# Pooled attention and a gated MLP on one core: K's left-over rows in one transfer, V's beside them at half the width

## The chip, the cores and the metric

The kernel runs on one core of one Trainium2 chip. The time is the device time of one execution in microseconds; a kernel is judged by the median of its runs, and one execution is taken apart with the hardware profiler. Engines: PE (matrix products, with weight loads on PEld), DVE (VectorE), ACT (ScalarE), POOL (GpSimd), SP (which issues nearly all the DMAs). Each engine works through its own list of instructions in a fixed order.

## The reference

All inputs are float32 but `w_in` and `w_out`, which are float64. B = 8 batches, H = 8 heads, S = 576 positions, D = 64.

```
k_p = k.reshape(B, H, 72, 8, D).mean(axis=3)         # eight positions pooled into one
v_p = v.reshape(B, H, 72, 8, D).mean(axis=3)
scores = (q @ k_p.T) / sqrt(D)                       # 576 x 72 for each head
attn = softmax(scores)
x = (attn @ v_p) as [B, S, H * D]                    # 512 columns

h = gelu_tanh(x @ w_in)                              # 1024 columns
u, v = h[..., :512], h[..., 512:]
v_n = (v - mean(v)) / sqrt(var(v) + 1e-6) * g_ln
v_s = einsum('ts,bsd->btd', w_sg, v_n) + b_sg        # w_sg is 576 x 576, over the positions
out = x + (u * v_s) @ w_out
```

## The kernel before

**Products.** Each float32 operand of a product in the second half is split into a high and a low float32r part (`xhl` holds both for x, `vhh` and `vhl` for v, `wih` and `wil` for `w_in`, `woh` and `wol` for `w_out`, `wsh` and `wsl` for `w_sg`, `ah` and `al` for the transposed softmax, `ghi` and `glo` for the gated product), and three of the four cross products are formed. A split is a cast on ACT or DVE and a subtraction on DVE or POOL. The float64 weights are cut into such pairs by integer operations on the raw words (`step_w`: tiles `raw`, `top`).

**Pooling.** The 72 pooled keys of a pair of heads are 144 rows of 8 x 64 numbers: 128 fill the partitions (`kvraw`, two transfers a batch for K and two for V, pooled into `kp` and `vp`), 16 are left over. The four pairs' left-over rows go into a tile of their own, `left`, and are pooled into `lp`. Eight values are summed in `psum8`, either by one reduction of DVE over the whole row, or by three additions of POOL, each over half the length of the one before: 512, 256 and 128 numbers for `kvraw` and for `left` (two halves side by side). K and V of the first two batches are pooled by PE instead (`pool8`), but not their left-over rows. V's left-over means are multiplied by a mask of heads into `left` again (or, for the first two batches, into the tile `vl`), and are split into `vl` from there.

**Scores.** K's means are turned and written, scaled, into `kbd`, a tile with the two heads of a pair on the block diagonal: for batches 0 and 1 by PE transposes, later by DVE transposes (`y`), a round trip through DRAM (`kfar`) and five ACT operations. PE multiplies `kbd` by `qT`; DVE takes the maxima (`nmax`), ACT the exponentials with their sums (`e`, `ssum`), DVE scales `e`, which goes transposed into `ah` and `al` for the product with V.

**Order.** The work of a batch is cut into steps, and a table, `PROLOGUE`, lists which step issues its next piece: `K1+2` is step K, part 1, of batch 2. A and B load K and V, E the left-over rows, C loads q; K and P pool K and V (K2 the left-over rows and `kbd`, P2 V's mask and splits), Q makes `qT`, S scores and softmax, T and L the transposed softmax, V the product with V, H the v half of `x @ w_in` with its norm, U the u half, W the spatial gate, O the product with `w_out`, X and Z the output; small letters are the splits of the weights. A second table, `OTHER`, names operations that go to the other of two engines. The rule for sums is

```
def psum8(o, t, key):
    if key not in OTHER:  # three additions on GpSimd
        ...
    nc.vector.tensor_reduce(...)  # else one on VectorE
```

with `k31` for the second half of K from batch 3 on, `k20` for the first of batch 2, `l1` and `l2` for the left-over rows of batches 1 and 2 (`l3` from there on). For copies a key in `OTHER` means DVE instead of ACT (`K00` for pooled K of batch 0, `Q02` for `qT`, `T00` for `ah`, `s1` for `wsh`, `H23` for `vhh`), for low parts of v (`H20`) DVE instead of POOL, and for `xta`, a copy of x for the H step (`X20`), POOL instead of ACT.

**The end.** The last 64 positions of the last batch are formed apart, in `step_X`: two halves of 256 columns, 12 products each, an addition of x on DVE, and a store, the first on the SP queue and the second on ACT's.

Of the kernel before, what the change touches and what calls it, by code (L numbers as in the profile page):

```python
# [24 lines left out]
Q1+0 Q2+0 v0 S0+0 S1+0 v0 v1 Q2+0 S1+0 C3+0 S0+0 S1+0 Q3+0 Q3+0 S2+0 lo0 v1 S0+0 S2+0 o1 S1+0 o0 A0+1 K1+1 o1 S2+0
S3+0 T0+0 B0+0 S3+0 o0 K1+1 S3+0 P0+0 E0+1 S2+0 S2+0 S3+0 lv1 S1+0 T0+0 S3+0 v2 P1+0 ls0 K0+1 P2+0 L0+0 o1 lu0 v3 K0+1
v2 v3 o1 s0 T1+0 K2+1 L0+0 s0 B0+1 s0 v3 V0+0 s4 T1+0 V1+0 v2 C0+1 V0+0 s4 T2+0 V1+0 s1 C1+1 K2+1 s4 s3 s1 v3 T2+0 s1
V0+0 Q0+1 K2+1 T3+0 V2+0 s3 v2 u1 u1 T3+0 V2+0 V3+0 S0+1 o0 C2+1 s2 Q1+1 B1+1 V3+0 V2+0 V1+0 u0 S1+1 o0 s2 V3+0 S0+1
u1 S0+1 s3 lu1 S1+1 s2 S1+1 H2+0 Q2+1 u1 S0+1 H0+0 u0 P0+1 S1+1 u0 H0+0 S2+1 P0+1 u0 H2+0 V1+0 H0+0 S2+1 u3 V2+0 C3+1
S2+1 V0+0 H2+0 P1+1 u3 lo1 S1+1 U1+0 U0+0 H2+0 H2+0 S0+1 H0+0 H0+0 V3+0 U1+0 H2+0 u2 U0+0 o2 H3+0 H0+0 Q3+1 S2+1 C1+2  # L30
H4+0 u2 A0+2 u3 u2 H3+0 P1+1 S3+1 o2 H4+0 T0+1 A1+2 H4+0 S3+1 o2 S3+1 u3 H1+0 u2 S3+1 P2+1 P2+1 U3+0 o2 S3+1 H1+0 S2+1
T0+1 T0+1 L0+1 P2+1 P2+1 U2+0 C0+2 L0+1 K1+2 H4+0 T1+1 L0+1 V0+1 T1+1 H1+0 E0+2 U3+0 H3+0 K0+2 H4+0 T1+1 V0+1 V1+1
B0+2 B1+2 H3+0 H1+0 T2+1 V1+1 T2+1 H1+0 H1+0 T3+1 T2+1 U2+0 Q1+2 V2+1 H3+0 T3+1 H3+0 H4+0 H4+0 P1+2 V1+1 P0+2 T3+1
# [901 lines left out]
```

## Time and profile before

| | |
|---|---|
| median of three runs | 562.36 us (561.85, 562.36 and one of 3028.21) |
| the profiled execution, whole | 560.36 us |
| its span from first to last instruction | 558.7 us |
| instructions in it | 10694 |
| granted PE clock | 1.00 in every stretch |
| busy: PE, DVE, ACT, POOL | 538.1, 435.2, 330.6, 260.8 us |
| moved by DMA | 68.38 MB, 122 GB/s over the span |

A row of the timeline gives start, duration, engine, line, operation, what it writes and reads with shapes, and in square brackets the idle time before it with what ended it. A row of the groups gives line, engine, operation, shapes, count, then busy us and mean ns of one, then idle before. Shapes are partitions x elements. `xN` at the end of a timeline row stands for N such instructions in a row, with their time together. Lines are those of the kernel that ran.

### The profile page before, as it was taken

The numbers are of one execution on the slowest core, as the hardware profiler recorded it, in microseconds if no ns is written. First come the engines' busy times: TensorE is split into PE (matmuls) and PEld (weight loads), VectorE is DVE, ScalarE is ACT, GpSimd is POOL, SyncE is SP. The second block draws the span as 40 slices with busy tenths as digits, with TensorE's granted clock in tenths as the row PEclk, the third lists the DMA queues.
The fourth block names the chain that finished last, engine by engine and source line by source line (L and its number), as shares of the span: only waits on it lengthen the run. The fifth ranks groups of instructions, "written<-read, shape, count | busy, mean of one in ns | idle before, by whom it ended". The sixth has DMA issues, their size and how long they took to land.

```text
span 558.7 us, 10694 instructions
## 1 busy us (share of the span) xinstructions
PE 538.1 (96%) x3677; PEld 508.7 (91%) x3677; DVE 435.2 (78%) x644; ACT 330.6 (59%) x1077; POOL 260.8 (47%) x322
## 2 busy tenths in 40 slices
...
GB/s 246 315 298 164 93 120 76 69 145 122 158 147 90 93 155 146 138 111 134 166 104 158 86 177 162 119 48 151 122 169 99 95 44 83 78 59 2 32 13 106
DMA packets 186470, 68.38 MB, mean 122 GB/s; under 512 B 150576, under 2 KB 170800, under 8 KB 186416
## 3 DMA queue, kind: packets, MB, share of 16 engines
...
HBM read 48.20 MB, written 19.46 MB: 121 GB/s over the span
## 4 chain that ended last, share of the span: by engine, by line
PE 78%; DVE 9%; ACT 4%; SPq 3%; DMA 3%; issue 1%; POOL 0%; DVEq 0%; ACTq 0%; POOLq 0%
PE mps L139 66%; PE aps L139 12%; SPq L240 3%; ACT e L564 2%; DMA kvraw<-in_k 1%; ACT L207 1%; DVE vg L739 1%; DVE bst L733 1%; DVE al L649 0%; DMA al<-tfar 0%; DVE top L237 0%; DMA lfar<-y 0%; DVE e L223 0%; DVE raw L228 0%; DVE wsl L320 0%
## 5 line engine op out<-in xcount | busy, mean ns | idle before, releaser
L564 ACT ACTIVATE e<-aps,nmax 128x72 f32<-128x72 f32 x280 | 85.0, 354 | 6.3 <-DVE nmax L545 6.2
L139 PE MATMUL mps<-xhl,wih 128*128 128x288 f32 x512 | 88.2, 294 | 0.0
L139 PE MATMUL mps<-wih,xhl 128*128 128x512 f32 x256 | 84.7, 396 | 0.6 <-DVE wsl L320 0.3
L139 PEld LDWEIGHTS mps<-xhl,wih 128*128 128x128 f32 x512 | 75.5, 188 | 1.0
L237 POOL TENSOR_TENSOR glo<-u,ghi 128x576 fp32r<-128x576 f32 x29 | 42.4, 1478 | 69.9 <-ACT ghi L214 35.5
L564 ACT ACTIVATION_READ_ACCUMULATOR e<-aps,nmax 128x1 f32 x280 | 67.4, 242 | 0.0
L237 POOL TENSOR_TENSOR xhl<-x,xhl 128x576 fp32r<-128x576 f32 x30 | 43.8, 1471 | 41.9 <-ACT xhl L692 37.6
L139 PEld LDWEIGHTS mps<-wih,xhl 128*128 128x128 f32 x256 | 48.1, 188 | 11.1 <-ACT u L771 0.7
L139 PE MATMUL mps<-wsh,vhl 128*128 128x288 f32 x256 | 55.1, 296 | 0.3 <-DVE vhl L237 0.3
L139 PE MATMUL mps<-xhl,wil 128*128 128x288 f32 x256 | 54.8, 295 | 0.0
L139 PE MATMUL mps<-wsl,vhh 128*128 128x288 f32 x256 | 54.8, 295 | 0.0
L139 PE MATMUL mps<-wsh,vhh 128*128 128x288 f32 x256 | 54.7, 295 | 0.0
L139 PE MATMUL mps<-ghi,woh 128*128 128x288 f32 (+1 forms) x232 | 51.8, 302 | 0.0
L139 PE MATMUL mps<-ghi,wol 128*128 128x288 f32 (+1 forms) x232 | 50.8, 298 | 0.0
L139 PE MATMUL mps<-glo,woh 128*128 128x288 f32 (+1 forms) x232 | 50.8, 298 | 0.0
L139 PE MATMUL mps<-wil,xhl 128*128 128x512 f32 x128 | 50.1, 391 | 0.0
L785 DVE SCALAR_TENSOR_TENSOR mps<-mps,gcol,bbc 128x576 f32<-128x576 f32 x32 | 26.2, 819 | 27.6 <-PE mps L139 27.6
L237 POOL TENSOR_TENSOR vhl<-vg,vhh 128x512 fp32r<-128x512 f32 x25 | 34.6, 1389 | 23.5 <-DVE vhh L212 18.6
L736 POOL TENSOR_TENSOR rstd<-mv,eps 128x1 f32<-128x1 f32 (+1 forms) x40 | 13.0, 325 | 68.8 <-DVE mv L734 65.5
L646 ACT CAST ah<-al 128x640 fp32r<-128x640 f32 x24 | 17.5, 731 | 41.6 <-DMA al<-tfar 37.9
L139 PEld LDWEIGHTS mps<-wsh,vhl 128*128 128x128 f32 x256 | 41.1, 188 | 0.6 <-DVE vhl L237 0.6
L139 PEld LDWEIGHTS mps<-wsh,vhh 128*128 128x128 f32 x256 | 41.2, 188 | 0.0
...
## 6 DMA issues: line engine op xcount, KB each, us to landing
...
```

The lines of the kernel that those rows point to most:

```text
L139: nc.tensor.matmul(o, lhsT, rhs, start=start, stop=stop)
L207: nc.scalar.activation(early, eps[:, 0:1], func)
L237: (nc.vector if key in OTHER else nc.gpsimd).tensor_tensor(o, x, y, op=op)
L240: queue.dma_start(o, i)
L564: nc.scalar.activation(e[:, i, h], slots[i][:, h], AF.Exp, bias=nmax[:, i, h:h + 1], **acc)
L646: nc.scalar.copy(ah, al)
L733: nc.vector.bn_stats(bst, vg)
L736: nc.gpsimd.tensor_tensor(rstd, mv[:, 1:2], eps[:n, 1:2], op=ALU.add)
L739: nc.vector.scalar_tensor_tensor(vg, vg, mv[:, 0:1], rstd.broadcast_to([n, DF2]), op0=ALU.subtract, op1=ALU.mult)
L785: nc.vector.scalar_tensor_tensor(vs, vs, gcol[:, d:d + 1], bbc.rearrange("p (a n) -> p a n", a=2), op0=ALU.mult, op1=ALU.add)
```

## The change

**Left-over rows.** `left` is [128, 1, 512] instead of [128, 2, 512]. K's 64 rows of a batch come in one transfer to partitions 64 to 127, V's in two transfers of 32 rows to partitions 0 to 31 and 32 to 63; before, each of the two had two transfers of 32 rows, side by side in the same partitions. `psum8` of them covers 128 partitions, with one row of 512 numbers in each instead of two rows in 64 partitions: additions of 256, 128 and 64 numbers. The transposes and the DRAM trip of `lp` are half as wide (128x64), `kbd` of batches 0 and 1 takes one ACT operation for the left-over part instead of two, V's mask two POOL operations of 32x256 in every batch instead of one of 32x512 from batch 2 on.

**Last rows.** In `step_X` each half of the columns has a PSUM tile of its own, and the first half is added and stored ahead of the second half's products.

**Order.** `PROLOGUE` is another list from its start to where batches 2 and 3 meet, and differs further in the last output steps only; `OTHER` is another list altogether.

```diff
...
-A0+0 K0+0 A1+0 E0+0 K0+0 lv0 K1+0 v1 v0 K2+0 K1+0 K2+0 K2+0 v1 C0+0 v0 Q0+0 C1+0 Q0+0 S0+0 A1+1 S0+0 C2+0 B1+0 Q1+0
...
+A0+0 K0+0 A1+0 E0+0 lv0 C0+0 v0 K1+0 C2+0 K2+0 K1+0 K0+0 K2+0 v1 K2+0 C1+0 v0 Q0+0 Q0+0 v1 S0+0 Q1+0 Q2+0 S0+0 v1 S0+0
...
-G01 G10 G23 H13 H23 Q01 Q02 Q03 V02 V12 W00 W10 W13 X02 X03 X10 X12 X13 X21 X22 c21 c22 g00 g10 g12 g13 g14 g21 g22
-h01 k31 l1 l2 o0d o2a o2m o3m p30 p31 u0m u1m u2a u2d u3a u3d u3m v0m v1m v2a v2d v2m v3a x11
+G00 G12 G23 H01 H02 H10 H11 H12 H20 H22 K00 Q01 T00 V01 V03 W00 W02 W03 W13 X00 X03 X11 X12 X13 X20 X22 X23 c21 c22
+g11 g13 g22 h00 h11 h12 k20 o0m o1a o1d o1m o2d o2m o3d o3m p30 p31 s1 s2 u1d u2a u2d u2m u3m v0m v1d v2m x01 x12
...
     nc.gpsimd.affine_select(out=head[:, 1:2], in_=head[:, 1:2], compare_op=ALU.is_ge, fill=0.0, base=-SP,
                             pattern=[[0, 1]], channel_multiplier=1)
-    pick = const.tile([96, 2, NL], F32, name="pick")
-    mask = const.tile([96, 2, 2], F32, name="mask")
+    pick = const.tile([64, 2, 2 * NL], F32, name="pick")
+    mask = const.tile([64, 2, 2], F32, name="mask")
     nc.gpsimd.memset(pick, 1.0 / POOL)
     nc.gpsimd.memset(mask, 0.0)
-    sl = pick[64:96]
-    nc.gpsimd.affine_select(out=sl, in_=sl, compare_op=ALU.is_equal, fill=0.0, base=0,
-                            pattern=[[-1, 2], [-2, NL]], channel_multiplier=1)
-    nc.vector.tensor_reduce(out=mask[64:96, :, 1], in_=sl, axis=AX.X, op=ALU.add)
+    nc.gpsimd.affine_select(out=pick, in_=pick, compare_op=ALU.is_equal, fill=0.0, base=0,
+                            pattern=[[-1, 2], [-2, 2 * NL]], channel_multiplier=1)
+    nc.vector.tensor_reduce(out=mask[:, :, 1], in_=pick, axis=AX.X, op=ALU.add)
     kbd = const.tile([P, G, 2 * SP], F32, name="kbd")
     nc.gpsimd.memset(kbd, 0.0)
     vbh = const.tile([P, G, P], F32R, name="vbh")
...
     nc.gpsimd.tensor_copy(swap[:, 0:P // 2], ident[:, P // 2:P])
     nc.gpsimd.tensor_copy(swap[:, P // 2:P], ident[:, 0:P // 2])
     lp = const.tile([P, 2, D], F32, name="lp")
-    nc.gpsimd.memset(lp[0:64], 0.0)
+    nc.gpsimd.memset(lp[:, 1], 0.0)
     def turn(ps, src):
...
     def load_left(b):
-        t = per.tile([P, 2, POOL * D], F32, name="left")
-        for p0, src in ((96, k), (64, v)):
-            for gp in range(2):
-                load(t[p0:p0 + 32, gp], keys(src[b])[2 * gp:2 * gp + 2, P:2 * SP].rearrange("g r f -> r g f"))
+        t = per.tile([P, 1, POOL * D], F32, name="left")
+        load(t[64:P, 0], keys(k[b])[:, P:2 * SP].rearrange("g r f -> r g f"))
+        for gp in range(2):
+            load(t[32 * gp:32 * gp + 32, 0], keys(v[b])[2 * gp:2 * gp + 2, P:2 * SP].rearrange("g r f -> r g f"))
         st["left", b] = t
     def load_q(b, g):
...
                 psum8(kp, st.pop(("kv", b, 0, i)), f"k{min(b, 3)}{i}")
             return
         st["lp", b] = lp
-        psum8(lp[64:P], st["left", b][64:P], f"l{min(b, 3)}")
+        psum8(lp[:, 0:1], st["left", b], f"l{min(b, 3)}")
         yield
         kp = st.pop(("kp", b))
         c = D ** -0.5 / POOL
         if b not in BY_PE:
-            t = ring(per, [P, 2, 6, 32], "y", 2)
-            for n0, x in ((0, kp), (G, lp)):
+            t = ring(per, [P, 2, G + 1, 32], "y", 2)
+            for n0, x in ((0, kp), (G, lp[:, 0:1])):
                 nc.vector.transpose(t[:, :, n0:n0 + x.shape[1]].rearrange("p f g j -> p g f j"),
                                     x.rearrange("p g (f k) -> p g f k", k=32))
-            far = hbm.tile([P, 2, 6, 32], F32, name="kfar")
+            far = hbm.tile([P, 2, G + 1, 32], F32, name="kfar")
             load(far, t)
             yield
             far = far.rearrange("(q k) f g j -> k f q (g j)", k=32)
...
             for f in range(2):
                 r = slice(32 * f, 32 * f + 32)
                 load(kt[r], far[:, f, :, 0:P])
-                load(kl[r], far[:, f, 3, P:P + 64])
+                load(kl[r].rearrange("k (q j) -> k q j", q=2), far[:, f, 2:4, P:P + 32])
             yield
             kt = kt.rearrange("p q (g j) -> p g q j", g=G)
             m = SP - 64
...
             nc.scalar.mul(kbd[0:D, :, 64:SP], kt[:, :, 2, 0:m], c)
             nc.scalar.mul(kbd[D:P, :, SP:96], kt[:, :, 2, m:32], c)
             nc.scalar.mul(kbd[D:P, :, 96:P], kt[:, :, 3], c)
-            nc.scalar.mul(kbd[D:P, :, P:2 * SP].rearrange("p (f g) r -> p f g r", g=2),
-                          kl.rearrange("p (f r g) -> p f g r", f=2, g=2), c)
+            nc.scalar.mul(kbd[D:P, :, P:2 * SP], kl.rearrange("p (r g) -> p g r", g=G), c)
             return
         ps = atile()
         for g in range(G):
...
         main = ps[0:D, 0].rearrange("p (g j) -> p g j", g=G)
         nc.scalar.mul(kbd[0:D, :, 0:SP], main[:, :, 0:SP], c)
         nc.scalar.mul(kbd[D:P, :, SP:P], main[:, :, SP:P], c)
-        for gp in range(2):
-            nc.scalar.mul(kbd[D:P, 2 * gp:2 * gp + 2, P:2 * SP],
-                          ps[D * gp:D * gp + D, 1, 96:P].rearrange("p (r g) -> p g r", g=2), c)
+        nc.scalar.mul(kbd[D:P, :, P:2 * SP], ps[0:D, 1, 64:P].rearrange("p (r g) -> p g r", g=G), c)
     vb = {b: per.tile([P, G, P], F32, name="vb", tag=("vht", "al")[b]) for b in WHOLE}
...
                 psum8(vp, st.pop(("kv", b, 1, i)), f"p{min(b, 3)}{i}")
             return
         vp = st.pop(("vp", b))
-        vlp = st.pop(("lp", b))[64:96]
+        vlp = st.pop(("lp", b))[0:64, 0:1]
         left = st.pop(("left", b))
-        v32 = left[64:96, :, 0:4 * D].rearrange("p g (a d) -> p g a d", a=4)
+        v32 = left[64:96, 0].rearrange("p (g a d) -> p g a d", g=2, a=4)
         for h in range(2):
             nc.scalar.mul((vb[b] if b in WHOLE else vbh)[:, :, D * h:D * h + D], vp, head[:, h:h + 1])
-        heads = mask[64:96].rearrange("p g h -> p (g h)").unsqueeze(1).unsqueeze(3)
-        if b in TURNED:
-            for gp in range(2):
-                nc.gpsimd.tensor_tensor(st["vl", 0][64 + 32 * gp:96 + 32 * gp, gp:gp + 1],
-                                        vlp[:, gp:gp + 1].unsqueeze(2).broadcast_to([32, 1, 4, D]),
-                                        heads.broadcast_to([32, 1, 4, D]), op=ALU.mult)
-            if b in WHOLE:
-                return
-        else:
-            nc.gpsimd.tensor_tensor(v32, vlp.unsqueeze(2).broadcast_to([32, 2, 4, D]),
-                                    heads.broadcast_to([32, 2, 4, D]), op=ALU.mult)
+        heads = mask.rearrange("p g h -> p (g h)").unsqueeze(1).unsqueeze(3)
+        for gp in range(2):
+            r = slice(32 * gp, 32 * gp + 32)
+            nc.gpsimd.tensor_tensor(st["vl", 0][64 + 32 * gp:96 + 32 * gp, gp:gp + 1] if b in TURNED else v32[:, gp:gp + 1],
+                                    vlp[r].unsqueeze(2).broadcast_to([32, 1, 4, D]),
+                                    heads[r].broadcast_to([32, 1, 4, D]), op=ALU.mult)
+        if b in WHOLE:
+            return
         yield
         for h in range(2):
             r = slice(D * h, D * h + D)
...
         x = per.tile([n, DM], F32, name="xrow", tag="qraw1")
         copy(x, ps, "Z0")
         yield
-        ps = mtile()[0:n]
-        part = [slice(DM // 2 * k, DM // 2 * (k + 1)) for k in range(2)]
+        y = per.tile([n, DM], F32, name="yrow", tag="qraw0")
+        w = DM // 2
         for k in range(2):
+            ps = (mtile, atile)[k]()[0:n, 0, 0:w]
+            cols = slice(w * k, w * (k + 1))
             for c in range(KC):
-                for j, (w, z) in enumerate([(woh, ghi), (wol, ghi), (woh, glo)]):
-                    mm(ps[:, k, 0:DM // 2], z[:, c, LAST:S], w[:, c, part[k]], c == 0 and j == 0,
-                       c == KC - 1 and j == 2)
-            yield
-        y = per.tile([n, DM], F32, name="yrow", tag="qraw0")
-        for k in range(2):
-            nc.vector.tensor_tensor(y[:, part[k]], ps[:, k, 0:DM // 2], x[:, part[k]], op=ALU.add)
-            yield
-            load(out[b, LAST:S, part[k]], y[:, part[k]], (nc.sync, nc.scalar)[k])
+                for j, (r, z) in enumerate([(woh, ghi), (wol, ghi), (woh, glo)]):
+                    mm(ps, z[:, c, LAST:S], r[:, c, cols], c == 0 and j == 0, c == KC - 1 and j == 2)
+            yield
+            nc.vector.tensor_tensor(y[:, cols], ps, x[:, cols], op=ALU.add)
+            yield
+            load(out[b, LAST:S, cols], y[:, cols], (nc.sync, nc.scalar)[k])
             yield
     def store(b, m, y, t):
```

The places where the order moves follow, each before and then after; line numbers shift by up to eight between the two.

ACT from its first weight conversion to the exponentials of the first two pairs of batch 0, before (`mps` and `top` from `raw` are conversions of `w_in`'s words, `kp` from `aps` is the copy of pooled K):

```order
L285 ACTIVATE mps<-raw 128x512 x2
L214 COPY kp<-aps 128x128
L450 ACTIVATE kbd<-aps 64x4x72
L451 ACTIVATE kbd<-aps 64x4x56
L453 ACTIVATE kbd<-aps 64x2x16 x2
L214 COPY qT<-aps 128x576
L293 CAST wih<-top 128x512
L564 ACTIVATE e,ssum<-mps,nmax 128x72 x10
L293 CAST wih<-top 128x512
```

and after:

```order
L284 ACTIVATE mps<-raw 128x512
L213 COPY kp<-aps 128x128
L284 ACTIVATE mps<-raw 128x512
L448 ACTIVATE kbd<-aps 64x4x72
L449 ACTIVATE kbd<-aps 64x4x56
L450 ACTIVATE kbd<-aps 64x4x16
L213 COPY qT<-aps 128x576
L233 ACTIVATE raw<-raw 128x512
L292 CAST wih<-top 128x512
L557 ACTIVATE e,ssum<-mps,nmax 128x72 x10
L213 COPY qT<-aps 128x576
L284 ACTIVATE top<-raw 128x512
```

The copy of pooled K now stands between the two conversions, and a second copy of `qT` comes behind the first ten exponentials; a third one follows ten exponentials later.

DVE where batch 1's transposed softmax is split and the pooled K of batch 2 is turned, before (the rows of `al` are the second, third and fourth of the batch's four; `y` takes the turned K of batch 2):

```order
L635 TENSOR_TENSOR al<-aps,ah 128x576
L739 SCALAR_TENSOR_TENSOR vg<-vg,mv,rstd 128x512 x2
L212 COPY x_1077<-aps 128x576
L635 TENSOR_TENSOR al<-aps,ah 128x576
L528 STREAM_TRANSPOSE qT<-qraw 128x576
L739 SCALAR_TENSOR_TENSOR vg<-vg,mv,rstd 64x512
L635 TENSOR_TENSOR al<-aps,ah 128x576
L753 TENSOR_TENSOR vht<-vg,vht 64x512
L398 TENSOR_REDUCE lp<-left 64x128
L422 STREAM_TRANSPOSE y<-kp 128x4x2x32
L422 STREAM_TRANSPOSE y<-lp 128x2x2x32
```

and after:

```order
L628 TENSOR_TENSOR al<-aps,ah 128x576
L397 TENSOR_REDUCE kp<-kvraw 128x128
L211 CAST xhl<-aps 128x576
L628 TENSOR_TENSOR al<-aps,ah 128x576
L732 SCALAR_TENSOR_TENSOR vg<-vg,mv,rstd 128x512
L732 SCALAR_TENSOR_TENSOR vg<-vg,mv,rstd 64x512
L421 STREAM_TRANSPOSE y<-kp 128x4x2x32
L421 STREAM_TRANSPOSE y<-lp 128x2x32
L236 TENSOR_TENSOR vhl<-vg,vhh 128x512
L628 TENSOR_TENSOR al<-aps,ah 128x576
L746 TENSOR_TENSOR vht<-vg,vht 64x512
```

The sum of batch 2's left-over rows is gone from this list, a sum of half of its K (`kp` from `kvraw`) is in it, and both transposes stand between the third `al` and the fourth instead of behind the fourth.

PE between batch 1's product with V and the first scores of batch 2 (`kbd` and `qT`); a piece of the difference, with - for what stood there before only (`wth`, `wtl` are the last rows of `w_sg`):

```order
 L139 MATMUL mps<-wth,vht 128x288 x2
 L139 MATMUL mps<-wtl,vht 128x288 x2
-L139 MATMUL mps<-wsh,vhh 128x288 x2
-L139 MATMUL mps<-wsl,vhh 128x288 x2
-L139 MATMUL mps<-wsh,vhl 128x288 x2
...
-L139 MATMUL mps<-wth,vht 128x288 x2
-L139 MATMUL mps<-wtl,vht 128x288 x2
 L139 MATMUL aps<-kbd,qT 128x144 x10
```

Two quarters of the spatial gate of batch 0, 28 products each, lay between the two; now it is one, and the other follows behind the scores.

More of the change, by code (lines that the diff above doesn't have):

```diff
@@ L23 @@
 PROLOGUE = """
-A0+0 K0+0 A1+0 E0+0 K0+0 lv0 K1+0 v1 v0 K2+0 K1+0 K2+0 K2+0 v1 C0+0 v0 Q0+0 C1+0 Q0+0 S0+0 A1+1 S0+0 C2+0 B1+0 Q1+0
[L25 to L33, printed above, removed]
@@ new lines @@
+O0+0 O2+0 H0+1 V0+1 H3+1 Z2+0 Z2+0 H1+1 U0+1 S2+2 Z0+0 S2+2 S3+2 S1+2 S3+2 H0+1 Z0+0 S3+2 V1+1 O1+0 S2+2 H0+1 T0+2
+K1+3 L0+2 P2+2 U0+1 K0+3 O1+0 O1+0 H1+1 E0+3 T0+2 H1+1 U3+1 U3+1 H0+1 L0+2 L0+2 L0+2 H4+1 L0+2 H4+1 H4+1 H2+1 V0+2
+U2+1 H2+1 Z1+0 O3+0 H4+1 Q0+3 H4+1 T1+2 U2+1 H2+1 K2+3 T1+2 H4+1 O3+0 Z1+0 T2+2 H0+1 Q1+3 T1+2 H2+1 B0+3 V1+2 T2+2
+U1+1 O3+0 H0+1 H2+1 H2+1 H4+1 C2+3 H4+1 T2+2 T3+2 Z3+0 Z3+0 T2+2 K2+3 W1+1 V0+2 V2+2 U1+1 V1+2 T3+2 W0+1 W1+1 V1+2
+V2+2 T3+2 W2+1 K2+3 P0+3 T3+2 V3+2 B1+3 K2+3 V3+2 V2+2 C3+3 W0+1 W2+1 S0+3 V3+2 Q2+3 S0+3 S1+3 P1+3 W3+1 W1+1 V0+2
@@ new lines @@
+W0+1 S0+3 A0+4 S1+3 W3+1 W2+1 C0+4 Q3+3 V2+2 S1+3 S0+3 H2+2 W0+1 H2+2 P2+3 W2+1 W1+1 U2+2 H2+2 V3+2 S3+3 S1+3 V0+2
+S0+3 W3+1 O0+1 W3+1 S3+3 U2+2 S2+3 T0+3 S3+3 P2+3 O0+1 T1+3 S2+3 O1+1 O1+1 V1+2 P2+3 O0+1 S1+3 S3+3 T0+3 O2+1 S2+3
+S3+3 O2+1 O1+1 H1+2 Z1+1 T0+3 P2+3 H2+2 Z1+1 O2+1 O3+1 S2+3 O3+1 H1+2 S2+3 L0+3 Z2+1 Z2+1 H2+2 H0+2 H1+2 O3+1 L0+3
+H2+2 H0+2 K0+4 C1+4 H4+2 A1+4 L0+3 Q0+4 H4+2 T0+3 H0+2 U3+2 H4+2 L0+3 U3+2 T3+3 V0+3 H3+2 H1+2 H1+2 T1+3 H4+2 H1+2
+H3+2 E0+4 U1+2 T1+3 L0+3 U1+2 H4+2 U0+2 T2+3 H0+2 H4+2 H4+2 B0+4 Z0+1 Q1+4 T1+3 H0+2 H3+2 Z3+1 H0+2 H3+2 H4+2 K2+4
@@ new lines @@
+V1+3 T2+3 Z0+1 H3+2 V0+3 U0+2 H3+2 W0+2 T2+3 W2+2 K1+4 Z3+1 V1+3 W0+2 T2+3 V2+3 K2+4 T3+3 W2+2 W1+2 V2+3 P0+4 W3+2
+K2+4 W0+2 T3+3 W1+2 C3+4 T3+3 V3+3 W0+2 W1+2 B1+4 W2+2 V1+3 W2+2 K2+4 C2+4 V3+3 W3+2 S0+4 W3+2 S0+4 S1+4 P1+4 W1+2
+S0+4 W3+2 O0+2 Q3+4 P2+4 V3+3 V2+3 C1+5 V0+3 O1+2 O0+2 S0+4 S1+4 O0+2 O1+2 T0+4 S3+4 V2+3 O1+2 S3+4 A0+5 H1+3 S0+4
+O2+2 P2+4 S1+4 S1+4 V1+3 H1+3 S3+4 Q2+4 S2+4 O2+2 K0+5 S2+4 T0+4 O3+2 B0+5 S2+4 C0+5 H1+3 O2+2 V3+3 S1+4 O3+2 H2+3
+H1+3 T1+4 Z2+2 O3+2 S3+4 T0+4 Z2+2 S2+4 H0+3 P2+4 H2+3 S2+4 V0+3 U3+3 S3+4 L0+4 L0+4 H0+3 U2+3 H1+3 T0+4 U3+3 L0+4
```

88 lines of the change are left out of this document (41 added, 47 removed).

## Prediction

> **What bounds the kernel now.** I read the page first: the busy shares (part 1) and the chain that ended last (part 4).
>
> ```profile
> PE 538.1 (96%) x3677; PEld 508.7 (91%) x3677; DVE 435.2 (78%) x644; ACT 330.6 (59%) x1077; POOL 260.8 (47%) x322
> ...
> PE 78%; DVE 9%; ACT 4%; SPq 3%; DMA 3%; issue 1%; POOL 0%; DVEq 0%; ACTq 0%; POOLq 0%
> ```
>
> TensorE works 96% of the span, and the chain passes through it for 78%. GpSimd, the engine whose pooling steps are halved, has no share in the chain at all: what it saves is worth something only where somebody waits for it. An average hides stages, so next came the busy times by stretch (columns: length, then PE, PEld, DVE, ACT, POOL busy, granted clock, DMA share, GB/s).
>
> ```profile
> 16.75:31.69 14.94, 11.69 (x93) 10.53 (x91) 13.47 (x25) 14.71 (x86) 4.64 (x7) 1.00 1.06 336
> 31.69:92.81 61.12, 56.86 (x368) 50.04 (x368) 58.88 (x89) 55.34 (x162) 41.29 (x47) 1.00 0.50 130
> ...
> 92.81:200.00 107.19, 107.19 (x753) 103.43 (x753) 94.08 (x139) 68.86 (x244) 53.96 (x65) 1.00 0.51 121
> 200.00:493.00 293.00, 290.94 (x2011) 277.59 (x2009) 233.95 (x338) 174.24 (x555) 135.81 (x159) 1.00 0.52 122
> ```
>
> The rows name a different bound for each stage. To 31.69 it is ACT: 14.71 busy of 14.94, with the weights' and K's transfers beside it. From there to 92.81 it is VectorE: 58.88 of 61.12, while PE waits now and again. From 92.81 to 493 PE is busy for 398.13 of 400.19 us, so whatever other engines win or lose below their slack changes nothing there. Then the tail, where no work is left to overlap. So the change is priced at four places: start, VectorE's stretch, the middle, the tail.
>
> **The start (to 31.69).**
>
> ```profile
> 10.55 1.16 ACT L285 ACTIVATE mps<-raw 128x512 f32<-128x512 f32 x2 [2.01 <-DMA raw<-in_moe_w_in]
> 11.65 0.25 ACT L214 COPY kp<-aps 128x128 f32<-128x128 f32 x1
> ...
> 14.72 0.69 DVE L289 SCALAR_TENSOR_TENSOR raw<-top 128x512 int32<-128x512 int32 x1
> 15.81 0.91 DVE L545 TENSOR_REDUCE nmax<-mps 128x10 f32<-128x720 f32 x1 [0.40 <-PE mps L139]
> ...
> L214 ACT COPY qT<-aps 128x576 f32<-128x576 f32 x1 | 0.6, 638 | 0.0
> ```
>
> The copy of pooled K that the first scores need stands behind two weight conversions, 0.58 each; the new order puts it between them. K's left-over columns of `kbd` are also one ACT operation instead of two. Both would bring the first maxima (15.81) 0.55 or more forward, but VectorE's conversion ahead of them ends at 14.72 + 0.69 = 15.41: 0.40 is gained. Then ACT, full, takes two query copies from VectorE between the exponentials: 2 x 0.638 = 1.28. Its gap of 14.94 - 14.71 = 0.23 can take some. So the last scaling of batch 0, at 31.69 now, comes 1.28 - 0.40 - 0.23 = **+0.65** later.
>
> **VectorE's stretch (31.69 to 92.81).** It starts with that scaling and ends where PE gets the third `al` of batch 1.
>
> ```profile
> 92.01 0.75 DVE L635 TENSOR_TENSOR al<-aps,ah 128x576 fp32r<-128x576 f32 x1
> 92.81 0.40 PE L139 MATMUL aps<-ah,vbh 128*128 128x288 f32 x1
> ...
> DVE vg L723 <- ACT vg L721: 0.7, 1, 0.7
> ```
>
> The first is on VectorE, the second the product that it feeds; the third says that VectorE waited for another engine once in the stretch, 0.7 us. VectorE's forms (shape, count, busy us, mean ns, idle before):
>
> ```profile
> L739 DVE SCALAR_TENSOR_TENSOR vg<-vg,mv,rstd 128x512 f32<-128x512 f32 x32 | 26.3, 834 | 3.4 <-POOL rstd L737 3.1
> ...
> L528 DVE STREAM_TRANSPOSE qT<-qraw 128x576 f32<-128x576 f32 x28 | 21.3, 763 | 0.7 <-PE aps L139 0.7
> ...
> L398 DVE TENSOR_REDUCE kp<-kvraw 128x128 f32<-128x1024 f32 x5 | 10.0, 2000 | 0.0
> ...
> L212 DVE CAST vhh<-vg 128x512 fp32r<-128x512 f32 x16 | 8.3, 526 | 0.2
> ...
> L228 DVE SCALAR_TENSOR_TENSOR raw<-raw 128x512 f32<-128x512 uint32 x8 | 6.3, 786 | 0.0
> ...
> L237 DVE TENSOR_TENSOR vhl<-vg,vhh 128x512 fp32r<-128x512 f32 x7 | 5.6, 803 | 0.0
> ...
> L398 DVE TENSOR_REDUCE lp<-left 64x128 f32<-64x1024 f32 x2 | 4.0, 2006 | 0.1
> ...
> L237 DVE TENSOR_TENSOR wil<-raw,top 128x512 fp32r<-128x512 f32 x4 | 3.3, 829 | 0.2
> ...
> L237 DVE TENSOR_TENSOR xhl<-x,xhl 128x576 fp32r<-128x576 f32 x2 | 2.5, 1256 | 0.8 <-ACT x L214 0.8
> ...
> L212 DVE CAST xhl<-aps 128x576 fp32r<-128x576 f32 x1 | 0.7, 748 | 0.0
> ```
>
> I tallied VectorE's instructions from the last scaling of batch 0 to the third `al` of batch 1 in both orders. Gone: the left-over sum of batch 1 (2.006), three `wil` subtractions (3 x 0.829), one `vg` (0.834), one `vhh` (0.526): 5.85 us. New: a K sum of batch 2 (2.000), an `xhl` cast (0.748), a `raw` conversion (0.786), a `qT` transpose (0.763), a `vhl` subtraction (0.803), an `xhl` subtraction (1.256), two casts of `wsh` at 576 columns, for which the trace of before has no VectorE row; the nearest is the `xhl` cast of the same size, 0.748 each: 7.85 us. The queue is **+2.00** longer: the left-over sum did go to GpSimd, but more was put in its place. Against this stands VectorE's idle of 61.12 - 58.88 = 2.24. If none of it closes up, the full 2.00 comes late; if all of it, nothing (-0.24). I take the one named wait of 0.7 to close, since that work is in a new order, and as much again of the small gaps: 1.4. That leaves **+0.60**, with bounds -0.24 and +2.00.
>
> **`kbd` of batch 2: nothing.** Here the cover is thin.
>
> ```profile
> 98.63 0.27 DVE L422 STREAM_TRANSPOSE y<-lp 128x128 f32<-128x128 f32 x1
> ...
> 106.06 0.25 ACT L441 ACTIVATE kbd<-y 64x64 f32<-64x64 f32 x1
> ...
> 106.68 0.53 PE L139 MATMUL aps<-kbd,qT 128*128 128x144 f32 x3
> ```
>
> K leaves VectorE at 98.90, goes through DRAM, and ACT writes the last part of `kbd` at 106.31, 7.41 later; PE uses it 0.37 after that. In the order of before 104 matmuls lie between 92.81 and 106.68, 13.87 / 104 = 0.133 each. The new order leaves 76: a quarter of a spatial gate, 28 matmuls, comes later, so PE asks for `kbd` 28 x 0.133 = 3.7 earlier behind the third `al`. But the transposes moved up as well: two `vg` (one of them of 64 rows, counted alike) and K's own transposes lie between that `al` and their end, 2 x 0.834 + 0.27 and a wider one, some 2.5 us, where 98.90 - 92.76 = 6.1 lay before: 3.6 less. I take 0. A gain is excluded, since `kbd` holds nobody up now; at the other end the transposes come as late behind `al` as before, and PE waits 3.7 - 0.4 = 3.3.
>
> **The middle.** GpSimd's forms:
>
> ```profile
> L395 POOL TENSOR_TENSOR kvraw<-kvraw 128x512 f32<-128x512 f32 x9 | 12.7, 1414 | 7.9 <-DMA kvraw<-in_k 6.6 <-DMA kvraw<-in_v 1.2
> ...
> L395 POOL TENSOR_TENSOR kvraw<-kvraw 128x256 f32<-128x256 f32 x9 | 8.3, 922 | 0.7
> L395 POOL TENSOR_TENSOR left<-left 64x512 f32<-64x512 f32 x6 | 8.0, 1340 | 3.1 <-DMA left<-in_v 2.8
> L490 POOL TENSOR_TENSOR left<-lp,mask 32x512 f32<-32x512 f32 x6 | 6.5, 1089 | 0.5
> ...
> L395 POOL TENSOR_TENSOR left<-left 64x256 f32<-64x256 f32 x6 | 5.8, 959 | 0.5
> ...
> L396 POOL TENSOR_TENSOR lp<-left 64x128 f32<-64x128 f32 x6 | 3.9, 648 | 0.5
> ...
> L396 POOL TENSOR_TENSOR kp<-kvraw 128x128 f32<-128x128 f32 x7 | 3.6, 514 | 0.5
> L484 POOL TENSOR_TENSOR vl<-lp,mask 32x256 f32<-32x256 f32 x4 | 2.8, 691 | 0.3
> ```
>
> A left-over sum costs 1.340 + 0.959 + 0.648 = 2.95 a batch now. The time goes by elements in a row, not by rows: 64x256 takes 959, 128x256 takes 922. So 128x256 and 128x128 are 0.92 + 0.51; 128x64 has no row, above nothing and below 0.51, and at the falling steps I take 0.35: 1.8 us, **1.15 less** on GpSimd. In exchange VectorE's half of K's sum (2.0) becomes a GpSimd triple of 1.414 + 0.922 + 0.514 = 2.85 in five batches, and some `vhl` subtractions move the other way. The mask on V's left-over means, in two pieces of 32x256 instead of one of 32x512, adds 2 x 0.691 - 1.089 = 0.29. GpSimd has 135.81 busy of 293, VectorE 233.95, PE 290.94: the engine that bounds is not touched. SP issues three left-over transfers a batch instead of four, with 3% of the chain on all its issues. **0**; PE's idle of 2.06 is all that can be won, and as much I allow as loss.
>
> GpSimd now adds where VectorE reduced. By the Trainium skill ("GPSIMD Engine Reference", section "1. Specifications") GpSimd's way into SBUF is shared with VectorE, with contention for VectorE instructions of two SBUF inputs, which would let the added sums hold VectorE up.
>
> ```profile
> 301.11 4.22 POOL L237 TENSOR_TENSOR xhl<-x,xhl 128x576 fp32r<-128x576 f32 x3
> ...
> 304.22 1.14 DVE L571 TENSOR_TENSOR ssum<-ssum,eps 128x10 f32<-128x10 f32 x1 [0.99 <-ACT e L564]
> ```
>
> A two-input sum of ten columns takes 1.14 and ends at 305.36, just after GpSimd's three subtractions end at 305.33. The trace agrees with that rule here. By it the sum would be 1.8 higher, as the rival on the port works out from rows; without it nothing is added.
>
> **The tail.** The 64 last rows are stored in two halves.
>
> ```profile
> 555.06 0.76 DVE L847 TENSOR_TENSOR yrow<-mps,xrow 128x256 f32<-128x256 f32 x2 [1.44 <-PE mps L139]
> ...
> 555.85 0.36 ACTq L240 DMA_DIRECT2D out<-yrow  x1
> ```
>
> Both additions start after PE's last matmul, and the store that ends the kernel is issued behind the second. With a PSUM tile for each half the first addition runs while PE forms the second half. One addition goes from the end: 0.76 / 2 = **-0.38**. The span behind the issue stays.
>
> **Sum.** 0.65 + 0.60 + 0 + 0 - 0.38 = **+0.87**. The profiled execution took 560.36 (span 558.7), so it becomes 561.2; the median of the runs shown, 562.36, lies 2.0 above it, which gives **563.2**.
>
> **Rivals.** *VectorE's stretch gets shorter* (0.27). The left-over sum that goes (2.006) stands early in VectorE's queue, ahead of the splits that the first `x @ w_in` products wait for; what is added comes later. If PE, once early, is held by nothing (ACT with 55.34 of 61.12 is near its own limit, which speaks against), 2.0 of it stays: -2.0 - 0.38, so 560.0.
>
> *`kbd` of batch 2 late* (0.13). If the transposes or ACT's five `kbd` operations queue as long as before behind other work, PE waits for up to 3.3: 563.2 + 3.3 = 566.5; half of it 564.9. It decides when the last `kbd` operation ends later than 76 x 0.133 = 10.1 behind the third `al`. For it speaks the slack of 0.37.
>
> *K's second half late* (0.02), which ends on the other side. GpSimd's 2.85 stands in the path of K's way to `kbd`; if K's transposes waited for it in all of five batches, and nothing covered it, 5 x 2.85 = 14.3, so 577. It decides when the sums end behind VectorE's transposes; GpSimd's idle of over half the time speaks against.
>
> *The shared port* (0.05). If a VectorE instruction waits out the added GpSimd sums in its own stretch, one left-over sum, 1.8 us, comes back there as a loss: 565.0.
>
> *Pooling steps not half as long* (0.04): were the time set by rows, a triple would stay at 2.95 or grow. 959 against 922 speaks against it, and GpSimd's slack hides it: 563.2 again.
>
> **Chances.** My forecast 0.49, the rivals 0.27, 0.13, 0.02, 0.05, 0.04. Bounds of the forecast itself: 562.4 (all idle closes) to 564.6 (none). The range of 559.4 to 566.0 takes in the first rival, with the 0.6 by which the middle may help it, and most of the second; the upper part of the second, K late and stray cases are left out. Over 2% (11.2 us, about what a measurement can tell from no change) is reached only by K late, or by mishaps that no row points to: slower 0.03, faster 0.01, within 0.96.
>
> **What would show it.** Right: the scaling of batch 0 some 0.6 after 31.69; PE's third `al` product of batch 1 at 93 to 95 with VectorE busier than 58.88; sums of `left` at 128 rows near 0.9, 0.5 and 0.35; PE on `kbd` of batch 2 near 104 to 105 without a wait on ACT; end 0.4 earlier behind the last matmul. Wrong: PE there well before 92.8 (the first rival); a PE wait on `kbd` anywhere (the second and third); VectorE means above those of the rows quoted (the port).

## Result and profile after

The changed kernel takes **567.36 us** (median of six runs, 565.72 to 568.10), the kernel before 562.34 (six runs): 1.0092 of it, 95% interval 1.0073 to 1.0110, so 5.0 us slower. One of the six runs before took 3028.21 us; such stray runs, which a few of the sets below have too, are left out of the ratios. The forecast was 563.2, in a range from 559.4 to 566.0, so the kernel is 1.4 us slower than the range allowed. The sign of the likeliest case was right, its size was not: +0.87 against +5.0. The profiled execution took 567.37 (span 565.7).

Busy times and chain of the changed kernel, from its page:

```profile
PE 541.3 (96%) x3677; PEld 509.4 (90%) x3677; DVE 424.8 (75%) x644; ACT 332.7 (59%) x1073; POOL 264.4 (47%) x342
...
PE 70%; ACT 10%; DVE 8%; DMA 5%; SPq 3%; POOL 2%; issue 2%; DVEq 0%; ACTq 0%; POOLq 0%
```

VectorE has 10.4 us less to do than before, GpSimd 3.6 more. PE's share of the chain fell from 78% to 70%, and ACT, DMA and GpSimd came in: PE waits more often. The stretches that the prediction used, in the same columns:

```profile
31.69:92.81 61.12, 57.31 (x369) 49.68 (x367) 57.02 (x92) 52.76 (x156) 43.22 (x51) 1.00 0.48 125
92.81:200.00 107.19, 106.62 (x738) 102.84 (x738) 91.01 (x140) 69.76 (x244) 50.62 (x64) 0.98 0.50 116
200.00:493.00 293.00, 288.11 (x1975) 273.15 (x1974) 223.83 (x333) 173.23 (x549) 136.92 (x172) 1.00 0.50 120
```

VectorE was not busier in its stretch but less busy (57.02, 58.88 before). From 92.81 to 200, with PE full before, the mean granted clock is 0.98 and 738 instead of 753 matmul records fall in. From 200 to 493 PE is idle for 4.89 instead of 2.06. What it waits for there, before and then after (a row gives what waits, on what, the us in all, how often, and the longest):

```profile
PE aps L139 <- DVE e L223: 1.0, 1, 1.0
PE mps L139 <- POOL xta L218: 0.4, 1, 0.4
PE mps L139 <- DVE vhl L237: 0.3, 1, 0.3
PE mps L139 <- ACT u L771: 0.3, 1, 0.3
```

```profile
PE mps L139 <- DVE vhl L236: 2.1, 3, 1.1
PE aps L139 <- DVE e L222: 1.3, 1, 1.3
PE aps L139 <- ACT x L684: 0.7, 1, 0.7
PE mps L139 <- ACT vg L722: 0.6, 1, 0.6
PE aps L139 <- DVE lt L614: 0.2, 1, 0.2
```

The low part of v (`vhl`) makes PE wait longer than before, and its gelu (`vg`) and the copy of x are new on the list.

### The profile page after: what moved, and what is told of

Same layout as the page of the kernel before. It is cut to its first block, busy times and chain, and to the rows that moved or that the text cites. A ratio compares the mean times of both kernels' runs of the same rounds, so it can differ in the third digit from the quotient of the medians.

```text
span 565.7 us, 10702 instructions
## 1 busy us (share of the span) xinstructions
PE 541.3 (96%) x3677; PEld 509.4 (90%) x3677; DVE 424.8 (75%) x644; ACT 332.7 (59%) x1073; POOL 264.4 (47%) x342
## 4 chain that ended last, share of the span: by engine, by line
PE 70%; ACT 10%; DVE 8%; DMA 5%; SPq 3%; POOL 2%; issue 2%; DVEq 0%; ACTq 0%; POOLq 0%
PE mps L139 58%; PE aps L139 11%; ACT e L557 4%; SPq L239 3%; ACT L206 2%; DMA raw<-in_moe_w_in 2%; DMA al<-tfar 1%; DVE bst L726 1%; DMA stage<-in_moe_w_sg 1%; DMA left<-in_k 1%; ACT vg L722 1%; DVE vg L732 1%; POOL rstd L730 1%; DVE vhl L236 1%; POOL rstd L729 1%
## 5 line engine op out<-in xcount | busy, mean ns | idle before, releaser
L236 POOL TENSOR_TENSOR glo<-u,ghi 128x576 fp32r<-128x576 f32 x28 | 41.1, 1484 | 56.3 <-ACT ghi L213 40.8
L139 PEld LDWEIGHTS mps<-wsl,vhh 128*128 128x128 f32 x256 | 41.2, 190 | 0.0
```

The source lines that it names most:

```text
L139: nc.tensor.matmul(o, lhsT, rhs, start=start, stop=stop)
L236: (nc.vector if key in OTHER else nc.gpsimd).tensor_tensor(o, x, y, op=op)
```

## Experiments

My theory after these lines: the two tables (order, engines) cost the time, above all the entries that move work between VectorE and GpSimd, and the new layout of the left-over rows costs nothing. The rival: the layout itself. Times below are medians of 4 to 12 runs. Each set was run beside the kernel before on one chip, and the ratios are to those runs; the sets come from four chips, on which the kernel before had medians from 562.16 to 562.41.

**Layout alone, and tables alone.** First: the changed kernel's functions, `PROLOGUE` and `OTHER` of before.

```diff
-PROLOGUE, OTHER of the changed kernel
+PROLOGUE, OTHER of before
```

> The changed kernel's left-over layout and last rows, under the order table and the engine table of before. Theory (the tables cost the time, the layout is free): the tail's 0.4 less than before, 561.5 to 562.5, and no PE wait on vhl above 0.5 us between 200 and 493. Rival (the layout itself, its 128-partition sums or its transfers, costs it): 566 to 568, as the changed kernel.

Measured **561.29**, ratio 0.9987 (0.9977 to 0.9997). Second, the functions of before under the new tables:

```diff
-PROLOGUE, OTHER of before
+PROLOGUE, OTHER of the changed kernel
```

> The left-over layout and last rows of before, under the order table and the engine table of the changed kernel. GpSimd then forms the left-over sums of every batch from rows twice as long. Theory (the tables): 566 to 569, as slow as the changed kernel or slower. Rival (the layout): 561.5 to 563.

Measured **569.19**, ratio 1.0119 (1.0100 to 1.0137). Both are as the theory had it: the layout gains about 1 us under the old tables (562.27 - 561.29 = 1.0); under the new ones it is 1.8, though there the intervals of the two versions overlap. The tables lose 6 to 7.

**One table at a time.** With the new layout, first the new `OTHER` with the old `PROLOGUE`, then the reverse:

```diff
-PROLOGUE of the changed kernel
+PROLOGUE of before
```

> The changed kernel's layout under the order table of before, with the whole engine table of the changed kernel. If the engine table alone carries the loss: 565.5 to 568. If the order table does: 561 to 562.5.

```diff
-OTHER of the changed kernel
+OTHER of before
```

> The changed kernel's layout and order table, with the engine table of before. If the order table alone carries the loss: 565.5 to 568. If the engine table does: 561 to 562.5. Two tables that were made for each other may each be slower alone; then both this run and the one with the engine table alone lie above 563.

Measured **587.67** (1.0470, 1.0435 to 1.0506) and **577.53** (1.0269, 1.0237 to 1.0302). Each table alone is worse than both together, as the last case of the second expectation had it, and by far more than the other cases allowed. So the loss can't be shared out between them, only between places. That was done next.

**Start and middle.** The order from batch 3 on is the same in both tables but for the last output steps. Eight entries of `OTHER` that act there differ, and I counted seven: `H23` was left out. It is not the key of the cast `vhh`, as I wrote above (that one is `g23`), but of the low part `vhl` of the fourth block of 128 rows. Of the four blocks' `vhl`, from batch 2 on, one was on VectorE before (`H23`) and two are after (`H20`, `H22`). The seven others were set as in the changed kernel under the old tables, and as before in the changed kernel. So the first run below has three blocks on VectorE, and the second, called the old middle from here on, has none (19 and 5 such subtractions on VectorE in their profiles; 7 before, 17 after):

```diff
 OTHER of before, the layout of the changed kernel
-X21 g21 k31
+H20 H22 X20 X23
```

> The changed kernel's layout with both tables of before, but the seven entries that set the engines from batch 2 on as in the changed kernel: low parts of v of two row blocks on VectorE, K's second half on GpSimd, copies of x for two blocks on GpSimd and one on ACT, one cast of v on ACT. The order from batch 3 on is the same in both kernels. Theory (these entries cost the middle): 561.3 plus about 4.5, so 565 to 566.5. Rival (the middle suffers from the state in which the new start leaves the engines): 561 to 562.5.

```diff
 OTHER of the changed kernel
-H20 H22 X20 X23
+X21 g21 k31
```

> The changed kernel with those seven entries as before: new start, old middle. Theory (the entries cost the middle): the start's loss alone, 562.5 to 564. Rival (the start's state): 565.5 to 567.5.

Measured **564.14** and **566.14**. The seven entries cost 564.14 - 561.29 = 2.85 behind the old start. Behind the new one the difference is 567.36 - 566.14 = 1.2, which is not clear of the noise (intervals 1.0073 to 1.0110 and 1.0046 to 1.0095). The new start, with `H23`'s block on GpSimd, costs 566.14 - 561.29 = 4.85, far more than the theory had for it. Both theory and rival hold in part.

**Which entry of the middle.** In the changed kernel, one at a time back to the engine of before:

```diff
 OTHER of the changed kernel
-H20 H22
```

> The changed kernel, only the low parts of v of the first and third 128 rows go back from VectorE to GpSimd from batch 2 on. Theory (these subtractions queue behind waiting instructions on VectorE, and PE waits for them): the three PE waits on vhl, 2.6 us by the alignment of the traces, go: 564.5 to 565.5. Rival (VectorE's load as such, or GpSimd's, sets the middle and the waits move elsewhere): 567 to 568.

```diff
 OTHER of the changed kernel
+k31
```

> The changed kernel, only the sum of K's second half from batch 3 on goes back from GpSimd to VectorE. Theory (K's sum on GpSimd is not what costs): 567 to 569, since VectorE gets 2.0 us more a batch. Rival (VectorE waits for GpSimd's K sums, which it did for 1.2 us in the trace, and what is queued behind comes late): 564.5 to 566.5.

Measured **567.14** and **569.44**. The waits on VectorE's `vhl` did go with the first, but the time did not: PE then waits on `vg` (1.2) and x (1.1), as the rival had it. With the second it became 2.1 slower. That isn't the middle's doing, as far as its one profile shows: from batch 3's product with V to the last matmul it takes 352.92, the changed kernel 352.90, and what it loses lies up to batch 1's product with V (96.03 against 93.41), ahead of any sum that the entry moves. Under the old tables the same entries were added singly (with `H23` kept, so that `vhl` has three blocks on VectorE):

```diff
 OTHER of before, the layout of the changed kernel
+H20 H22
```

> The layout under both tables of before, with the low parts of v of two row blocks on VectorE from batch 2 on. With all seven entries of the middle it took 564.14, without them 561.29. If these two carry it: 563 to 564.5, with PE waits on vhl of 1.5 to 2.5 in all. If K's sum or the copies of x do: 561 to 562.

```diff
 OTHER of before, the layout of the changed kernel
-k31
```

> The layout under both tables of before, with only the sum of K's second half from batch 3 on moved to GpSimd. If GpSimd's longer sums hold up VectorE's transposes or its two-input instructions: 562.5 to 564. If they hide in GpSimd's idle time, and VectorE's 2.0 a batch hide too: 561 to 562. If VectorE's load is what bounds: 559.5 to 560.5.

Measured **563.20** and **563.93**: 1.9 and 2.6 above 561.29, together more than all seven (2.85). With the first, PE's waits on `vhl` come to 1.0 only, less than expected, with 0.8 on `vg` beside them. K's second half on GpSimd was the step that I had priced at 0, so this one is looked at closely. Its profile has two waits of PE that the run without the move doesn't have. First the layout under the old tables, VectorE around batch 7's K, and in the last row PE, which takes that `vhl`:

```profile
400.18 2.00 DVE L397 TENSOR_REDUCE kp<-kvraw 128x128 f32<-128x1024 f32 x1
402.22 0.89 DVE L614 TENSOR_TENSOR lt<-y,lt 32x640 fp32r<-32x640 f32 x1
403.21 0.45 DVE L421 STREAM_TRANSPOSE y<-kp 128x256 f32<-128x256 f32 x1
...
408.09 0.65 DVE L236 TENSOR_TENSOR vhl<-vg,vhh 128x512 fp32r<-128x512 f32 x1
...
408.80 0.54 PE L139 MATMUL mps<-wsh,vhl 128*128 128x288 f32 x2
```

The same place with that sum on GpSimd (GpSimd's row, then VectorE's two, then PE's):

```profile
401.76 2.59 POOL L394 TENSOR_TENSOR kvraw<-kvraw 128x512 f32<-128x512 f32 x2
...
404.92 0.45 DVE L421 STREAM_TRANSPOSE y<-kp 128x256 f32<-128x256 f32 x1 [1.19 <-POOL kp L395]
...
410.37 0.65 DVE L236 TENSOR_TENSOR vhl<-vg,vhh 128x512 fp32r<-128x512 f32 x1
...
411.07 0.53 PE L139 MATMUL mps<-wsh,vhl 128*128 128x288 f32 x2 [1.47 <-DVE vhl L236]
```

VectorE used the time in which ACT's `lt` was not ready to add up K. Now it idles there, waits 1.78 for `lt` and then 1.19 for K from GpSimd, and `vhl`, queued behind the transposes, is 2.3 later, in a version that had been 0.6 late before that place. PE had no room for it: without the move it took `vhl` at 408.80, 0.06 after its end at 408.74. GpSimd's idle time is of no use, since its queue came to that sum only after the normalising of v.

The other wait is at batch 6's K, on GpSimd, ACT and PE:

```profile
327.98 3.48 POOL L394 TENSOR_TENSOR kvraw<-kvraw 128x512 f32<-128x512 f32 x2
331.55 0.79 POOL L395 TENSOR_TENSOR kp<-kvraw 128x128 f32<-128x128 f32 x1
332.30 2.70 POOL L236 TENSOR_TENSOR vhl<-vg,vhh 128x512 fp32r<-128x512 f32 x2
...
333.79 0.60 ACT L722 ACTIVATE vg<-mps 128x512 f32<-128x512 f32 x1 [3.21 <-POOL vhl L236]
...
334.44 0.80 PE L139 MATMUL mps<-xhl,wih 128*128 128x288 f32 x4 [1.28 <-ACT vg L722]
```

Here the added sum stands in GpSimd's own queue ahead of `vhl`. ACT's gelu waits 3.21 for that `vhl`, PE 1.28 for the gelu; without the move the gelu ran at 331.68 without a wait. The two waits, 1.47 and 1.28, come to 2.75, close to the 2.6 of the medians; at the other three batches PE has no new wait.

**Which step of the start.** The traces put a wait of 1.8 us of ACT on VectorE just ahead of the third `al` of batch 1, shown below. Two entries were tried, each alone in the changed kernel:

```diff
 OTHER of the changed kernel
-k20
```

> The changed kernel, only the first half of batch 2's K sum goes back from VectorE to GpSimd. Theory (this 2.0 us reduction stands on VectorE ahead of the cast of x, for which ACT waits 1.8 us, then the third al and PE): the third product with V of batch 1 starts 1.0 to 1.5 earlier than 93.4, and the time is 565.5 to 566.5. Rival (the next link, PE's own order or the exponentials, holds it as late): 567 to 568.

```diff
 OTHER of the changed kernel
-h11
```

> The changed kernel, only the cast of x for the second pair of batch 1 goes from VectorE to ACT, where it stood before. The same theory (ACT's copy of x and the third ah wait for that cast behind the reduction): the wait of 1.8 on ACT goes, the third product with V starts 1.0 to 1.3 earlier, 566 to 567. Rival (ACT's queue is as late itself): 567 to 568.

Measured **567.34** and **565.47**. The reduction was not the link: without it ACT still waits 1.6 for the cast, and PE has a new wait of 1.5 for `vhl` at 97 us, where VectorE's two `vg` take 2.35 beside GpSimd's sum (1.40 in the changed kernel) and its transposes wait 0.36 for that sum. The cast is a link: with it on ACT, ACT waits for VectorE no more at that place, and the median is 1.9 lower (the intervals, 1.0034 to 1.0077 and 1.0073 to 1.0110, just touch). But the third product with V starts at 93.37 in that profile, and not 1.0 to 1.3 ahead of 93.41 as expected. What the cast is worth there is read better from the second product with V to the third: 3.78 us before, 4.60 in the changed kernel, 4.20 with the cast on ACT. So the cast explains 0.4 of 0.8.

Then the same cast with the old middle, and the query copies on VectorE besides:

```diff
 OTHER of the changed kernel
-H20 H22 X20 X23 h11
+X21 g21 k31
```

> The new start with the old middle (566.14), and the cast of x for the second pair of batch 1 on ACT again, which took 1.9 from the changed kernel. If the loss of the start and that of the middle add: 564.0 to 564.8. If the cast only mattered for what the middle then met: 565.5 to 566.5.

```diff
 OTHER as in the run above
+Q02 Q03
```

> As the run with the new start and that cast on ACT, and the query copies of the third and fourth pairs of batch 0 on VectorE again, as before. My term for them was 0.65 at the last scaling of batch 0. If it holds to the end: 0.5 to 1.0 less than that run, 563.2 to 564. If VectorE, which bounds the next stretch, has the copies back as a loss: the same or up to 1.0 more.

Measured **565.32** and **565.66**. The first lies between its two cases: with the old middle the cast gives 0.8 at most, which is not clear of the noise. The query copies give nothing.

**A better version.** The layout under the old tables, with one pair of the last steps exchanged as in the changed kernel:

```diff
-... Z3+7 X0+7 Z3+7 X0+7 X0+7 X0+7 X0+7
+... Z3+7 Z3+7 X0+7 X0+7 X0+7 X0+7 X0+7
```

> The layout under both tables of before, with only the last output steps in the order of the changed kernel (the last store of z ahead of the last-row steps). That kernel's end lies 3.5 behind its last matmul, the layout's under the old order 4.1. If the tail adds to the rest: 560.5 to 561.0, below both kernels. If the moved store only shifts the wait: 561.0 to 561.6.

Measured **560.73**, 0.9970 of the kernel before (0.9958 to 0.9982): the fastest of all. It lies 0.6 below the run without the exchange, but the two intervals touch, so the exchange itself is not shown.

## Why the prediction was wrong

The program passes four points in every version: the last scaling of batch 0 on VectorE; the third product with V of batch 1 on PE (`aps<-ah,vbh`, 92.81 before); the first such product of batch 3 (206.94 before); the last matmul. Read from the timeline of one profile each, the stretches in us:

| version | to scaling | to V of batch 1 | to V of batch 3 | to last matmul | to the end |
|---|---|---|---|---|---|
| before | 31.69 | 61.12 | 114.13 | 347.73 | 4.0 |
| layout, old tables | 31.28 | 61.31 | 114.13 | 348.77 | 4.1 |
| with `vhl` moved | 30.66 | 61.20 | 114.14 | 350.25 | 4.2 |
| with K's sum moved | 30.71 | 61.24 | 114.14 | 350.80 | 4.5 |
| **changed kernel** | 32.22 | 61.19 | 115.85 | 352.90 | 3.5 |
| `k20` back | 32.01 | 62.33 | 116.04 | 353.32 | 3.5 |
| `h11` back | 31.29 | 62.08 | 114.31 | 352.45 | 3.5 |
| old middle | 31.96 | 62.48 | 115.41 | 350.02 | 3.4 |
| old middle, `h11` back | 31.85 | 62.09 | 115.78 | 350.18 | 3.5 |

The first four rows have the same tables up to batch 2, and there the first stretch differs by 1.0 (by 1.5 with the run of the exchanged steps, 32.12); the second and third repeat to 0.2 and 0.01.

**The start (+0.65)** came out as 32.22 - 31.69 = 0.53 in the trace of the changed kernel. That is smaller than the spread of that stretch, so the term is not shown, and its closeness may be luck. Returning the query copies to VectorE did not bring the scaling forward (32.11 against 31.85 without), so that within this spread nothing bears out the reason that I gave.

**VectorE's stretch (+0.60).** The tally of the queue was not what counted. Its list of instructions agrees with the trace, but the durations did not stay: VectorE had 57.02 us to do where I had it above 58.88 (seven conversions `raw<-top` took 0.73 each instead of 0.92, four `vg` 0.74 instead of 1.01). And still the third `al` was late. The links of the changed kernel, on VectorE, ACT, ACT, VectorE and PE:

```profile
90.60 0.75 DVE L211 CAST xhl<-aps 128x576 fp32r<-128x576 f32 x1
...
91.38 0.64 ACT L213 COPY x<-aps 128x576 f32<-128x576 f32 x1 [1.77 <-DVE xhl L211]
91.92 0.65 ACT L213 CAST ah<-aps 128x576 fp32r<-128x576 f32 x1
...
92.59 0.76 DVE L628 TENSOR_TENSOR al<-aps,ah 128x576 fp32r<-128x576 f32 x1 [1.25 <-ACT ah L213]
...
93.41 0.41 PE L139 MATMUL aps<-ah,vbh 128*128 128x288 f32 x1 [0.57 <-DVE al L628]
```

The cast of x that was moved to VectorE is something ACT's next copy waits for, 1.77 us, and VectorE then waits for ACT. Work put on the engine that bounds the stretch turned into a round trip between two engines. I had counted the cast's 0.748 and missed who waits for it; as shown, it explains 0.4 of the 0.8 by which the third product is later behind the second, and what brings the rest stays open. In this profile the stretch is no longer than before (61.19 against 61.12), since its earlier part was shorter. Four other profiles with the same tables but for an entry or a few took 62.3 to 63.1 (the rows `k20` back and old middle, and 62.64 and 63.13 with `vhl` and K's sum back), so the term is +0.1 to +2.0, some +1.2 on average; its forecast of +0.60 lies inside that spread and is not shown either.

**`kbd` and up to batch 3 (0).** `kbd` itself was right: PE takes it up at 105.12 without a wait, where I had 104 to 105.

```profile
104.85 0.43 PE L139 MATMUL mps<-wtl,vht 128*128 128x288 f32 x2
105.12 0.65 PE L139 MATMUL aps<-kbd,qT 128*128 128x144 f32 x4
```

But the stretch grew by 1.7, and I had no term for it. After three waits of PE between 88 and 94 (1.13, 1.13 and 0.57) the granted clock of the changed kernel falls. In the columns of the stretches, with PE's busy time behind the length and the clock third from the end:

```profile
91.00:94.00 3.00, 1.36 (x9) 1.12 (x10) 1.75 (x4) 2.35 (x4) 1.52 (x3) 1.00 0.45 175
94.00:97.00 3.00, 3.00 (x16) 3.00 (x15) 2.94 (x7) 1.67 (x3) 1.01 (x1) 0.56 0.32 70
97.00:100.00 3.00, 3.00 (x22) 3.00 (x22) 2.90 (x4) 0.00 (x0) 3.00 (x3) 0.87 0.71 210
```

By the last two rows the fall takes away 3 x (1 - 0.56) + 3 x (1 - 0.87) = 1.7 us of full speed, as much as the stretch grew. Where it doesn't fall, the stretch is longer for other reasons. With the old middle (115.41), from whose run this row is, PE waits for the sum of v's last rows, which stands behind a late `lt` on VectorE:

```profile
147.96 0.80 PE L139 MATMUL mps<-xhl,wih 128*128 128x288 f32 x4 [0.86 <-DVE vg L716]
```

That is 0.86 of 1.28. With `k20` back it is the wait of 1.5 at 97 us. Only with `h11` back, and the new middle, is the stretch nearly as long as before (114.31); with the old middle `h11` does not shorten it (115.78). Whether these have one cause stays open.

**The middle (0, at most 2.06 either way)** is the step that failed most: 352.90 against 347.73 before and 348.77 for the layout under the old tables. Its reason was that GpSimd has half its time free and that VectorE, not bounding, gains. The runs with K's sum (+2.6) and with `vhl` (+1.9) show in its place that an engine's free time over 293 us says nothing of a queue: each moved step sits in a chain PE - ACT - VectorE - GpSimd - PE of a few microseconds. At batch 7 that chain had a slack of 0.06 us where I assumed the whole idle time, and the stretches of one batch differ enough that PE loses at some batches and not at others. The rival "K's second half late" (0.02, 577) had the right mechanism and too large a price: two of five batches pay, 2.6 and not 14.3. That holds under the old tables; in the changed kernel neither entry, taken back alone, gave the time back: with `vhl` back PE waits on `vg` and x instead, and with K's sum back the middle takes as long (352.92).

The runs don't settle how the 352.90 - 348.77 = 4.1 divides. In the profiles the old middle has 350.02 of it, so the seven entries account for 2.9 there, against 1.2 of the medians. The 1.25 that is left has no run of its own: `H23` alone is a rival that was not tried, and a late arrival from the start is another. The first rival (560.0) asked for a start that PE is not held up in; the changed kernel's was held up three times between 88 and 94.

**The shared port** (0.05, 565.0). That rival placed it in VectorE's stretch, beside the sums of left-over rows; it shows in the middle, beside another instruction. GpSimd, VectorE and PE of the changed kernel near 475 us:

```profile
475.30 1.38 POOL L236 TENSOR_TENSOR vhl<-vg,vhh 128x512 fp32r<-128x512 f32 x1 [0.55 <-ACT vhh L213]
...
475.45 1.77 DVE L236 TENSOR_TENSOR vhl<-vg,vhh 128x512 fp32r<-128x512 f32 x1
...
477.28 0.53 PE L139 MATMUL mps<-wsh,vhl 128*128 128x288 f32 x2 [1.06 <-DVE vhl L236]
```

The subtraction that takes 0.65 elsewhere takes 1.77 beside a GpSimd subtraction, and PE waits 1.06 for it. By the Trainium skill ("GPSIMD Engine Reference", section "1. Specifications") VectorE's instructions with two SBUF inputs contend with GpSimd for its way into SBUF; these rows agree. The new table has two blocks of `vhl` on each engine, and here two of them fall side by side. It is no general loss: the mean of VectorE's `vhl` is 0.806 after and 0.803 before, so the sign that I named for this rival, longer means on VectorE, is not there.

**The left-over sums** were mis-sized a little. GpSimd's forms after:

```profile
L394 POOL TENSOR_TENSOR left<-left 128x256 f32<-128x256 f32 x8 | 6.7, 836 | 2.5 <-DMA left<-in_v 2.5
L394 POOL TENSOR_TENSOR left<-left 128x128 f32<-128x128 f32 x8 | 6.5, 817 | 0.6
L395 POOL TENSOR_TENSOR lp<-left 128x64 f32<-128x64 f32 x8 | 3.2, 406 | 0.6
```

0.836 + 0.817 + 0.406 = 2.06 against 1.8 forecast and 2.95 before: shorter, not half. Where the layout's gain of 1.0 under the old tables arises is not shown: the one profile of that version is no shorter than that of before (spans 559.6 and 558.7), and the execution of before was 2.0 faster than its median.

**The tail (-0.38)** was right up to the last store's issue.

```profile
562.16 0.28 PE L139 MATMUL aps<-woh,glo 128*128 128x256 f32 x1
...
562.48 0.42 DVE L839 TENSOR_TENSOR yrow<-aps,xrow 128x256 f32<-128x256 f32 x1 [0.94 <-PE aps L139]
...
562.94 0.36 ACTq L239 DMA_DIRECT2D out<-yrow  x1
```

The last store is issued 0.78 behind the last matmul, 555.85 - 554.67 = 1.18 before: 0.40 less. The time from issue to end varies by more than that between versions (2.7 to 4.2), so the gain at the end is seen in the changed kernel (3.5 instead of 4.0 behind the last matmul) and not in the layout under the old tables (4.1).

The profiles of before and after differ by 7.0 in span, the medians by 5.0: the execution of before that was profiled lies 0.9 below the fastest of its timed runs, and the one after had the fallen clock. The four runs of the changed kernel with a mean clock of 0.996 or 0.997 took 567.35 to 568.10, the two at 1.00 took 565.72 and 566.65. By these two the loss without the fallen clock is nearer 4 than 5, though the kernel before has executions at 0.997 too.
